# A decode kernel's output projection: from transposed 4-column matmuls to row-major accumulation with padded stationary activations

## The chip, the cores and the metric

One core of a Trainium2 chip. The metric is device microseconds of one execution. A kernel runs several times; the text gives medians, and for comparisons a ratio, explained with the result.

Abbreviations of the profile: PE is TensorE (matmuls), PEld its weight loads, DVE VectorE, ACT ScalarE, POOL GpSimd, SP the engine whose queue issues nearly all transfers. "L526" is a source line of the kernel concerned, so the same operation has another number in another kernel: the PV matmuls are L526 before and L521 after. A stretch on TensorE is called cold where its granted clock was 0.5 and warm where it was 1.0: the 512-column PV matmuls were 427 ns apart cold and 215 warm.

## The reference, cut to what matters

One decode step for 4 sequences: attention over a window of 2048 cached positions (32 query heads on 16 cached heads of 128), its output projection, and beside it an MLP with a layer norm, all added to the input.

```python
def reference(A_x, A_k_cache, A_v_cache, A_wq, A_wo, B_x, B_w1, B_w2, B_w3, B_w4):
    xn = _layernorm(A_x)
    # A: q = xn @ wq; scores over the last 2048 of 8192 positions; softmax; o = p @ v
    a = o.reshape(4, 1, 32 * 128) @ A_wo              # [4, 4096] @ [4096, 576]
    # B, for S == 1: x1 = xn (the shifted parts are all padding)
    h2 = gelu(_layernorm(xn) @ B_w3) @ B_w4           # [4, 4608] @ [4608, 576]
    return A_x + a + xn + h2
```

With one position per sequence the token shift of B moves everything out, so w1 and w2 drop out of the result. What is left is about 87 MB of K, V and weights to read for very little arithmetic.

## The kernel before

K tiles are transposed on TensorE and multiplied with q; the softmax is done once per sequence; V tiles are multiplied with the probabilities, in batches of four heads ("PV batches", 512 columns; the last two batches of the last sequence have two heads, 256 columns). In the last sequence, where there is no further K to load, the w3, wo and w4 work runs between the PV batches.

The two products that end the kernel, `@ wo` and `@ w4`, add into one PSUM tile `accT` of the *transposed* result: a 128x128 piece of the weight is stationary, and the four activation columns stream past it. For each head or w4 chunk that is five matmuls, because 576 output columns are cut into pieces of 128:

```python
def pe_wo(h0, h1):
    for h in range(h0, h1):
        PE.wait(("wo", h // HPW))
        ...
        for dc, (c0, rows) in enumerate(DCH):          # five pieces of 128 of the 576 columns
            PE.op(lambda e, ...: e.matmul(
                out=accT[:, dc * B:(dc + 1) * B], lhsT=wo_sb[:, h * D + c0:h * D + c0 + 128],
                rhs=oT_sb[:, h * B:(h + 1) * B], ...))
# at the end: copy accT to SBUF, transpose it on TensorE in fp32, add the residual (xpx20), two output DMAs
```

Transfers go through one in-order queue. K and V land in rings of slots; a V load waits until the PV batch that last used its slot is done:

```python
NKS = 8                                # K slots
NVS = 12                               # V slots; one load fills two
...
if G >= ngr:                           # ngr = NVS // 2
    DQ.wait((which + "free", G - ngr))
sp_dma(dst, src, sems[G % ngr], key=(which + "ld", G))
```

The end of the last sequence is a list of steps in program order: a PV batch, then for the batch before it the `oT` step through VectorE and its `pe_wo`, then a group of w3 matmuls; after the last PV batch the six w4 blocks.

## Time and profile before

| | before |
|---|---|
| median of the first 4 runs | 236.9 us (235.74 to 239.19) |
| median of 16 runs, those known after the prediction included | 235.8 us |
| span of the execution shown by the profile | 235.8 us (its run took 237.65) |
| TensorE busy | 189.1 us, 80% |
| VectorE, ScalarE, GpSimd busy | 37%, 27%, 2% |
| moved by DMA | 87.6 MB, mean 372 GB/s |

A span is what the profile of one execution covers; the time of that run is some 1.7 to 1.9 us longer. The lines of the profile are in the prediction.

### The profile page before, as it was taken

The numbers are of one execution on the slowest core, as the hardware profiler recorded it, in microseconds if no ns is written. First come the engines' busy times: TensorE is split into PE (matmuls) and PEld (weight loads), VectorE is DVE, ScalarE is ACT, GpSimd is POOL, SyncE is SP. The second block draws the span as 40 slices with busy tenths as digits, with TensorE's granted clock in tenths as the row PEclk, the third lists the DMA queues.
The fourth block names the chain that finished last, engine by engine and source line by source line (L and its number), as shares of the span: only waits on it lengthen the run. The fifth ranks groups of instructions, "written<-read, shape, count | busy, mean of one in ns | idle before, by whom it ended". The sixth has DMA issues, their size and how long they took to land.

```text
span 235.8 us, 6622 instructions
## 1 busy us (share of the span) xinstructions
PE 189.1 (80%) x3091; PEld 147.1 (62%) x3091; DVE 87.4 (37%) x208; ACT 63.8 (27%) x67; POOL 5.4 (2%) x9
## 2 busy tenths in 40 slices
PE   0399778779979597799999759999984595797885
PEld 0299778766857485668769447768662342536674
DVE  4435334552543425517437342536434110202110
ACT  7234253641531330415225043225221200000000
POOL 8000000000000000000000000000000000000000
PEclk9999889988999978789999985999998578757575
DMA  6999999999999999999999999999999999999960
GB/s 205 382 366 378 382 350 396 411 409 406 408 409 407 405 404 409 408 409 409 407 406 400 410 408 410 407 407 409 405 397 336 346 349 343 369 361 375 338 225 4
DMA packets 31240, 87.61 MB, mean 372 GB/s; under 512 B 1496, under 2 KB 10220, under 8 KB 31212
## 3 DMA queue, kind: packets, MB, share of 16 engines
q1 hardware_dynamic: 31196, 87.18, 98.1%
q8 instruction: 24, 0.39, 0.7%
q14 instruction: 4, 0.03, 0.0%
q10 hardware_dynamic: 16, 0.01, 0.0%
HBM read 87.17 MB, written 0.00 MB: 370 GB/s over the span
## 4 chain that ended last, share of the span: by engine, by line
PE 48%; DMA 34%; DVE 9%; SPq 4%; ACT 3%; issue 1%; ACTq 0%
DMA k_ring<-in_A_k_cache_dram 20%; PE pvb_ps L526 18%; PE ktp L455 17%; DMA v_ring<-in_A_v_cache_dram 8%; DMA wA<-in_A_wq_dram 6%; PE st_ps L496 5%; SPq L274 4%; DVE otmp L541 4%; PE st_ps L594 2%; DVE kt_sb L468 2%; PE st_ps L574 2%; PE st_ps L427 1%; DVE part_sb L683 1%; ACT L331 1%; ACT L299 1%
## 5 line engine op out<-in xcount | busy, mean ns | idle before, releaser
L455 PE MATMUL ktp<-ident_bf,k_ring 128*128 128x128 bf16 x1024 | 86.5, 235 | 6.3 <-DMA k_ring<-in_A_k_cache_dram 5.6
L473 ACT ACTIVATE kt_sb<-ktp 128x1024 bf16<-128x1024 bf16 x51 | 52.1, 1024 | 93.8 <-PE ktp L455 93.8
L526 PE MATMUL pvb_ps<-v_ring,pT_sb 128*128 128x512 bf16 (+1 forms) x272 | 69.0, 417 | 5.2 <-DMA v_ring<-in_A_v_cache_dram 5.2
L455 PEld LDWEIGHTS ktp<-ident_bf,k_ring 128*128 128x128 bf16 x1024 | 67.0, 105 | 9.6 <-DMA k_ring<-in_A_k_cache_dram 5.9
L468 DVE COPY kt_sb<-ktp 128x1024 bf16<-128x1024 bf16 x77 | 52.5, 690 | 41.2 <-PE ktp L455 41.1
L526 PEld LDWEIGHTS pvb_ps<-v_ring,pT_sb 128*128 128x128 bf16 x272 | 28.7, 110 | 37.8 <-issue 15.5
L496 PE MATMUL st_ps<-qT_sb,kt_sb 128*128 128x2 bf16 x1024 | 44.5, 165 | 2.8 <-ACT kt_sb L473 2.3
L541 DVE TENSOR_SCALAR otmp<-pvb_ps,rrs 128x128 bf16<-128x128 f32 x64 | 18.1, 344 | 77.0 <-PE pvb_ps L526 72.2
L496 PEld LDWEIGHTS st_ps<-qT_sb,kt_sb 128*128 128x128 bf16 x1024 | 40.1, 99 | 5.0 <-ACT kt_sb L473 2.7
L615 ACT ACTIVATE gT_sb<-ktp 128x36 bf16<-128x36 f32 x4 | 0.8, 201 | 32.2 <-PE ktp L610 32.2
L654 ACT ACTIVATE pT_sb<-st_ps 128x512 bf16<-128x512 f32 x4 | 2.4, 597 | 23.7 <-PE st_ps L678 23.7
L574 PE MATMUL st_ps<-oT_sb,wo_sb 128*128 128x4 bf16 x160 | 4.9, 165 | 4.2 <-DVE oT_sb L559 4.2
L574 PEld LDWEIGHTS st_ps<-oT_sb,wo_sb 128*128 128x128 bf16 x160 | 4.4, 98 | 4.6 <-DVE oT_sb L559 4.6
L352 PE MATMUL misc_ps<-ident_bf,xn_pad 128*128 128x128 bf16 x5 | 0.7, 302 | 8.2 <-DVE xn_pad L335 8.2
L686 PE MATMUL misc_ps<-ones_f,part_sb 128*128 128x1 f32 x8 | 1.9, 312 | 5.6 <-DVE part_sb L683 5.6
L554 PE MATMUL misc_ps<-imask,otmp 128*128 128x8 bf16 (+1 forms) x64 | 4.2, 168 | 2.5 <-DVE otmp L541 2.5
L610 PE MATMUL ktp<-uT_sb,wA 128*128 128x4 bf16 x180 | 5.3, 165 | 0.5 <-DMA wA<-in_B_w_dram 0.5
L610 PEld LDWEIGHTS ktp<-uT_sb,wA 128*128 128x128 bf16 x180 | 5.1, 101 | 0.8 <-issue 0.5
L686 PEld LDWEIGHTS misc_ps<-ones_f,part_sb 128*128 128x128 f32 x8 | 1.6, 250 | 6.4 <-DVE part_sb L683 6.4
L352 PEld LDWEIGHTS misc_ps<-ident_bf,xn_pad 128*128 128x128 bf16 x5 | 0.5, 129 | 8.2 <-issue 8.2
L554 PEld LDWEIGHTS misc_ps<-imask,otmp 128*128 128x128 bf16 x64 | 3.3, 100 | 3.5 <-DVE otmp L541 2.8
L683 DVE TENSOR_REDUCE part_sb<-pT_sb 128x32 f32<-128x512 bf16 x4 | 4.0, 1000 | 1.3 <-ACT pT_sb L654 1.3
(69 smaller groups left out, 54.8 us busy)
## 6 DMA issues: line engine op xcount, KB each, us to landing
k_ring<-in_A_k_cache_dram SPq DMA_DIRECT2D x32, 1024.0 KB, 15.2
v_ring<-in_A_v_cache_dram SPq DMA_DIRECT2D x32, 1024.0 KB, 17.7
wo_sb<-in_A_wo_dram SPq DMA_DIRECT2D x4, 1152.0 KB, 19.2
wA<-in_B_w_dram SPq DMA_DIRECT2D x4, 1152.0 KB, 15.4
wA<-in_A_wq_dram SPq DMA_DIRECT2D x4, 1024.0 KB, 12.0
k_ring<-in_B_w_dram SPq DMA_DIRECT2D x2, 1296.0 KB, 16.4
k_ring<-in_B_w_dram SPq DMA_DIRECT2D x1, 1440.0 KB, 18.4
kt_sb<-in_B_w_dram SPq DMA_DIRECT2D x1, 720.0 KB, 11.3
```

Source lines behind the costliest of these rows:

```text
L274: DQ.ops.append(("op", lambda e, o=out_ap, i=in_ap, s=s: e.dma_start(o, i).then_inc(s, 16), False))
L455: PE.op(lambda e, tt=tt, t=t, src=src, bank=bank: e.transpose(out=bank[:, tt * 128:(tt + 1) * 128], in_=src[:, t * 128:(t + 1) * 128], ide ...
L468: DVE.op(lambda e: e.tensor_copy(out=dst, in_=src), mark=("evac", c))
L473: ACT.op(lambda e: e.activation(out=dst, in_=src, func=ACTF.Copy), mark=("evac", c))
L496: PE.op(lambda e, t=t, src=src, hl0=hl0, b=b, stb=stb, st0=(first_of_b and tt == 0): e.matmul(out=stb[:, t * HL + hl0:t * HL + hl0 + REP], ...
L526: PE.op(lambda e, t=t, vs0=vs0, npr=npr, bank=bank: e.matmul(out=bank[:, 0:npr * 128], lhsT=pT_sb[:, t, :], rhs=v_ring[:, vs0:vs0 + npr, t ...
L541: DVE.op(lambda e, jj=jj, j=j, bank=bank: e.tensor_scalar(out=otmp[:, j, :], in0=bank[:, jj * 128:(jj + 1) * 128], scalar1=rrs32[:, 0:1], ...
L554: PE.op(lambda e, j=j, jj=jj, c0=c0, c1=c1, npr=npr: e.matmul(out=misc[:, OTF + c0:OTF + c1], lhsT=otmp[:, j, :], rhs=imask[:, j, c0:c1], ...
L574: PE.op(lambda e, h=h, dc=dc, c0=c0, st0=st0: e.matmul(out=accT[:, dc * B:(dc + 1) * B], lhsT=wo_sb[:, h * D + c0:h * D + c0 + 128], rhs=o ...
L594: PE.op(lambda e, fc=fc, dc=dc, c0=c0, last=last, st0=st0: e.matmul(out=accT[:, dc * B:(dc + 1) * B], lhsT=w4_chunk(fc, c0, 128), rhs=gT_s ...
L610: PE.op(lambda e, ff=ff, fc=fc, dc=dc, bank=bank: e.matmul(out=bank[:, ff * B:(ff + 1) * B], lhsT=wA[:, dc, fc * 128:(fc + 1) * 128], rhs= ...
L683: DVE.op(lambda e: e.tensor_reduce(out=part_sb[:, 0:HL], in_=pT_sb[:, :, 0:HL].rearrange("p t h -> p h t"), axis=AX.X, op=ALU.add), mark=( ...
```

## The change

Its intent: keep the activation stationary and let the weight stream. One head then takes two matmuls of 288 columns instead of five weight loads with 4 columns each, the result comes out in row order, and the final transpose goes. So that the stationary operand is a full 128 columns, the 4 activation columns are padded with zeros; the pads take 17 KB a partition, and the V ring pays for them.

```diff
-    NVS = 12 if NP >= 12 else NP
+    NVS = 8 if NP >= 8 else NP
...
+    DH0 = ((D + 1) // 2 + 31) // 32 * 32 if D > 512 else D
+    ACC_SPLIT = [(0, min(D, DH0))] + ([(DH0, D)] if D > DH0 else [])      # 0:288, 288:576
...
-        oT_sb = ent(nc.sbuf_tensor("oT_sb", [128, HQ * B], BF))
-        gT_sb = ent(nc.sbuf_tensor("gT_sb", [128, FC * B], BF))
+        oT_pad = ent(nc.sbuf_tensor("oT_pad", [128, HQ, 128], BF))
+        gT_pad = ent(nc.sbuf_tensor("gT_pad", [128, FC, 128], BF))
...
+        POOL.op(lambda e: e.memset(oT_pad[:, :, :], 0.0))
+        POOL.op(lambda e: e.memset(gT_pad[:, :, :], 0.0), mark="pmem")
...
-                for dc, (c0, rows) in enumerate(DCH):
-                    PE.op(... out=accT[:, dc * B:(dc + 1) * B], lhsT=wo_sb[:, h * D + c0:h * D + c0 + 128],
-                              rhs=oT_sb[:, h * B:(h + 1) * B] ...)
+                acc_mm(oT_pad[:, h, :], lambda n0, n1, h=h: wo_sb[:, h * D + n0:h * D + n1], False)
...
-            NHB = min(3, NKB)
+        NHB = NKB - 1                                     # banks for the w3 matmuls
...
-        DVE.op(... tensor_copy(out=accT_sb ...)); PE.op(... transpose ...); DVE.op(... add xpx20 ...)
+        for ai, (n0, n1) in enumerate(ACC_SPLIT):
+            DVE.op(... tensor_tensor(out=out_sb[:, n0:n1], in0=accs[ai][0:B, 0:n1 - n0], in1=xpx[:, n0:n1], op=ALU.add))
+        tiny_dma(out.rearrange("b s d -> (b s) d"), out_sb[:, :], s_out, key="out")
```

Cut: five small DMAs that brought the residual into the transposed layout, the memsets of tiles that no longer exist, and waits on the neighbouring wo or w4 block, which a 128-wide piece of the last 64 columns used to read into.

More of the change, by code (lines that the diff above doesn't have):

```diff
@@ L135, in bass_parallel_sum__sliding_block_cached__mixer_s_mlp__decode_kernel @@
     KT_ELEMS = NKT * NT * 128
-    NW4A = min(FC, (KR_ELEMS - 128) // D)
+    NW4A = min(FC, KR_ELEMS // D)
     NW4B = FC - NW4A
-    W4_SEP = not (NW4B * D + 128 <= KT_ELEMS or NW4B == 0)
+    W4_SEP = not (NW4B * D <= KT_ELEMS or NW4B == 0)
     if W4_SEP:
@@ L165, in bass_parallel_sum__sliding_block_cached__mixer_s_mlp__decode_kernel @@
     WA_COLS = max(HQ * DH, F)
+    DH0 = ((D + 1) // 2 + 31) // 32 * 32 if D > 512 else D
+    ACC_SPLIT = [(0, min(D, DH0))] + ([(DH0, D)] if D > DH0 else [])
+    assert all(n1 - n0 <= 512 for n0, n1 in ACC_SPLIT)
     def chunk_info(c):
@@ L186, in bass_parallel_sum__sliding_block_cached__mixer_s_mlp__decode_kernel @@
         wA = ent(nc.sbuf_tensor("wA", [128, NDC, WA_COLS], BF))
-        wo_sb = ent(nc.sbuf_tensor("wo_sb", [128, HQ * D + 128], BF))
+        wo_sb = ent(nc.sbuf_tensor("wo_sb", [128, HQ * D], BF))
         ident_bf = ent(nc.sbuf_tensor("ident_bf", [128, 128], BF))
         ones_bf = ent(nc.sbuf_tensor("ones_bf", [128, 128], BF))
-        ident_f = ent(nc.sbuf_tensor("ident_f", [128, 128], F32))
         identrep = ent(nc.sbuf_tensor("identrep", [128, NT * HL], BF))
@@ L195, in bass_parallel_sum__sliding_block_cached__mixer_s_mlp__decode_kernel @@
         xpx = ent(nc.sbuf_tensor("xpx", [B, D], F32))
-        xpx20 = ent(nc.sbuf_tensor("xpx20", [NR, 128], F32))
         bst1 = ent(nc.sbuf_tensor("bst1", [B, 12], F32))
@@ L216, in bass_parallel_sum__sliding_block_cached__mixer_s_mlp__decode_kernel @@
         imask = ent(nc.sbuf_tensor("imask", [128, HKV, 128], BF))
-        oT_sb = ent(nc.sbuf_tensor("oT_sb", [128, HQ * B], BF))
-        gT_sb = ent(nc.sbuf_tensor("gT_sb", [128, FC * B], BF))
-        accT_sb = ent(nc.sbuf_tensor("accT_sb", [128, 128], F32))
-        out20 = ent(nc.sbuf_tensor("out20", [NR, 128], BF))
-        w4_buf = ent(nc.sbuf_tensor("w4_buf", [128, FC * D + 128], BF)) if W4_SEP else None
+        oT_pad = ent(nc.sbuf_tensor("oT_pad", [128, HQ, 128], BF))
+        gT_pad = ent(nc.sbuf_tensor("gT_pad", [128, FC, 128], BF))
+        out_sb = ent(nc.sbuf_tensor("out_sb", [B, D], BF))
+        w4_buf = ent(nc.sbuf_tensor("w4_buf", [128, FC * D], BF)) if W4_SEP else None
         ktp = [ent(nc.psum_tensor("ktp%d" % i, [128, 1024], BF)) for i in range(NKB)]
@@ L230, in bass_parallel_sum__sliding_block_cached__mixer_s_mlp__decode_kernel @@
         ktp_f = [t[:, :].bitcast(F32) for t in ktp]
-        accT = st[B % 2]
-        outT = ktp_f[NKB - 1]
+        accs = [st[B % 2][:, :], ktp_f[NKB - 1]]
+        NHB = NKB - 1
+        assert NHB >= 1 and len(ACC_SPLIT) <= len(accs)
         assert NDC * 128 <= 1024
@@ L251, in bass_parallel_sum__sliding_block_cached__mixer_s_mlp__decode_kernel @@
         s_pe, s_dve, s_act, s_pool = sem("c_pe"), sem("c_dve"), sem("c_act"), sem("c_pool")
-        s_x, s_out, s_xpx = sem("d_x"), sem("d_out"), sem("d_xpx")
+        s_x, s_out = sem("d_x"), sem("d_out")
         s_wq = [sem("d_wq%d" % i) for i in range(NQB)]
@@ L291, in bass_parallel_sum__sliding_block_cached__mixer_s_mlp__decode_kernel @@
         DVE.op(lambda e: e.memset(rrs32[:, :], 0.0))
-        DVE.op(lambda e: e.memset(negm_bc[:, :], 0.0))
-        DVE.op(lambda e: e.memset(accT_sb[:, :], 0.0))
-        DVE.op(lambda e: e.memset(xpx20[:, :], 0.0))
-        if W4_SEP:
-            DVE.op(lambda e: e.memset(w4_buf[:, FC * D:FC * D + 128], 0.0))
-        DVE.selfsync(lambda e: e.memset(wo_sb[:, HQ * D:HQ * D + 128], 0.0), "dmem")
+        DVE.selfsync(lambda e: e.memset(negm_bc[:, :], 0.0), "dmem")
         if REM > 0:
@@ L309, in bass_parallel_sum__sliding_block_cached__mixer_s_mlp__decode_kernel @@
             mark="identrep")
-        POOL.op(lambda e: e.affine_select(
-            out=ident_f[:, :], in_=ones_bf[:, :], pattern=[[1, 128]],
-            compare_op=ALU.is_equal, fill=0.0, base=0, channel_multiplier=-1), mark="identf")
         POOL.wait("identbf")
@@ L558, in pe_oTacc, with acc_mm @@
             DVE.wait(("oTacc", n))
+            DVE.wait("pmem")
             DVE.op(lambda e, b=b, c0=c0, c1=c1: e.tensor_copy(
-                out=oT_sb[:, :].rearrange("p (h b) -> p h b", b=B)[:, c0:c1, b], in_=misc[:, OTF + c0:OTF + c1]),
-                mark=("oTb", n))
-        acc_started = [False]
+                out=oT_pad[:, c0:c1, b], in_=misc[:, OTF + c0:OTF + c1]), mark=("oTb", n))
+        acc_started = [False] * len(ACC_SPLIT)
+        def acc_mm(lhsT, rhs_fn, last):
+            for ai, (n0, n1) in enumerate(ACC_SPLIT):
+                st0 = not acc_started[ai]
+                acc_started[ai] = True
+                fin = last and ai == len(ACC_SPLIT) - 1
+                PE.op(lambda e, ai=ai, n0=n0, n1=n1, st0=st0, fin=fin: e.matmul(
+                    out=accs[ai][:, 0:n1 - n0], lhsT=lhsT, rhs=rhs_fn(n0, n1), start=st0, stop=fin,
+                    skip_group_check=True), mark=("acc" if fin else None))
         def pe_wo(h0, h1):
-            PE.wait("dmem")
+            PE.wait("pmem")
             for h in range(h0, h1):
                 PE.wait(("wo", h // HPW))
-                if REM > 0 and h + 1 < HQ:
-                    PE.wait(("wo", (h + 1) // HPW))
-                for dc, (c0, rows) in enumerate(DCH):
-                    st0 = not acc_started[0]
-                    acc_started[0] = True
-                    PE.op(lambda e, h=h, dc=dc, c0=c0, st0=st0: e.matmul(
-                        out=accT[:, dc * B:(dc + 1) * B], lhsT=wo_sb[:, h * D + c0:h * D + c0 + 128],
-                        rhs=oT_sb[:, h * B:(h + 1) * B], start=st0, stop=False, skip_group_check=True))
-        blk_of_fc = {}
-        for i_, (region_, f0_, n_) in enumerate(w4_blocks):
-            for fc_ in range(f0_, f0_ + n_):
-                blk_of_fc[fc_] = i_
+                acc_mm(oT_pad[:, h, :], lambda n0, n1, h=h: wo_sb[:, h * D + n0:h * D + n1], False)
         def pe_w4mm(i, last_block):
@@ L585, in pe_w4mm @@
             PE.wait(("w4", i))
+            PE.wait("pmem")
             for fc in range(f0, f0 + n):
                 PE.wait(("gelu", fc // FPB))
-                if REM > 0 and fc + 1 < FC and w4_blocks[blk_of_fc[fc + 1]][0] == region:
-                    PE.wait(("w4", blk_of_fc[fc + 1]))
-                for dc, (c0, rows) in enumerate(DCH):
-                    last = (last_block and fc == f0 + n - 1 and dc == NDC - 1)
-                    st0 = not acc_started[0]
-                    acc_started[0] = True
-                    PE.op(lambda e, fc=fc, dc=dc, c0=c0, last=last, st0=st0: e.matmul(
-                        out=accT[:, dc * B:(dc + 1) * B], lhsT=w4_chunk(fc, c0, 128),
-                        rhs=gT_sb[:, fc * B:(fc + 1) * B], start=st0, stop=last, skip_group_check=True),
-                        mark=("acc" if last else None))
+                acc_mm(gT_pad[:, fc, :], lambda n0, n1, fc=fc: w4_chunk(fc, n0, n1 - n0),
+                       last_block and fc == f0 + n - 1)
         def pe_h2T(j):
@@ L614, in pe_h2T @@
             ACT.wait(("h2T", j))
-            ACT.op(lambda e, j=j, bank=bank: e.activation(out=gT_sb[:, j * FPB * B:(j + 1) * FPB * B],
-                                                          in_=bank[:, 0:FPB * B], func=ACTF.Gelu_apprx_tanh),
-                   mark=("gelu", j))
+            ACT.wait("pmem")
+            ACT.op(lambda e, j=j, bank=bank: e.activation(
+                out=gT_pad[:, j * FPB:(j + 1) * FPB, 0:B], in_=bank[:, 0:FPB * B].rearrange("p (f b) -> p f b", b=B),
+                func=ACTF.Gelu_apprx_tanh), mark=("gelu", j))
         q_done = set()
@@ L661, in bass_parallel_sum__sliding_block_cached__mixer_s_mlp__decode_kernel @@
                     dma_wo(j)
-            if b == 0:
-                SP.wait("xpx")
-                SP.wait("dmem")
-                for dc, (c0, rows) in enumerate(DCH):
-                    tiny_dma(xpx20[dc * B:(dc + 1) * B, 0:rows], xpx[:, c0:c0 + rows], s_xpx)
-                EV["xpx20"] = (s_xpx, 16 * dma_counts[s_xpx.num])
             g0_chunks = list(range(c1_lo, c1_lo + CPG)) if nxt else []
@@ L761, in bass_parallel_sum__sliding_block_cached__mixer_s_mlp__decode_kernel @@
         DVE.wait("acc")
-        DVE.op(lambda e: e.tensor_copy(out=accT_sb[:, 0:NR], in_=accT[:, 0:NR]), mark="accTsb")
-        PE.wait("accTsb")
-        PE.wait("identf")
-        PE.op(lambda e: e.transpose(out=outT[:, 0:128], in_=accT_sb[:, :], identity=ident_f[:, :]), mark="outT")
-        DVE.wait("outT")
-        DVE.wait("xpx20")
-        DVE.op(lambda e: e.tensor_tensor(out=out20[:, :], in0=outT[0:NR, 0:128], in1=xpx20[:, :], op=ALU.add),
-               mark="fin")
-        SP.wait("fin")
-        out2 = out.rearrange("b s d -> (b s) d")
-        if NFULL > 0:
-            tiny_dma(out2[:, 0:NFULL * 128].rearrange("b (c p) -> c b p", p=128), out20[0:NFULL * B, :], s_out)
-        if REM > 0:
-            ACT.wait("fin")
-            act_dma(out2[:, NFULL * 128:D], out20[NFULL * B:NR, 0:REM], s_out)
-        EV["out"] = (s_out, 16 * dma_counts[s_out.num])
+        for ai, (n0, n1) in enumerate(ACC_SPLIT):
+            DVE.op(lambda e, ai=ai, n0=n0, n1=n1: e.tensor_tensor(
+                out=out_sb[:, n0:n1], in0=accs[ai][0:B, 0:n1 - n0], in1=xpx[:, n0:n1], op=ALU.add),
+                mark=("fin" if ai == len(ACC_SPLIT) - 1 else None))
+        SP.wait("fin")
+        tiny_dma(out.rearrange("b s d -> (b s) d"), out_sb[:, :], s_out, key="out")
         SP.wait("out")
```

## The prediction

> **What bounds the kernel now.** I read the page's slices first, then the chain of waits for the last 48 us, then a table of stretches cut at the PV batches, then the issue queue's order of time.
>
> ```profile
> PEclk9999889988999978789999985999998578757575
> DMA  6999999999999999999999999999999999999960
> GB/s 205 382 366 378 382 350 396 411 409 406 408 409 407 405 404 409 408 409 409 407 406 400 410 408 410 407 407 409 405 397 336 346 349 343 369 361 375 338 225 4
> ```
>
> Transfers are saturated in every slice from 6 us to about 224 us: some 408 GB/s while K and V stream, 336 to 375 in the last batch, where w3, wo and w4 share the queue. Until there the loads set the pace. Only the last slices are different, and there the clock reads 5 to 8.
>
> ```profile
> 188.11 18.50 DMA v_ring<-in_A_v_cache_dram
> 206.60 0.14 issue
> 206.74 6.10 PE pvb_ps L526 x16
> 212.84 0.02 issue
> 212.86 1.13 DVE otmp L541 x4
> 213.99 0.09 DVE oT_sb L559
> ...
> 226.15 0.66 PE st_ps L574 x20
> 226.80 1.25 PE st_ps L594 x50
> ...
> 228.37 0.66 PE st_ps L574 x20
> 229.03 3.48 PE st_ps L594 x130
> 232.51 0.02 issue
> 232.53 0.19 DVE accT_sb L762
> 232.72 0.04 issue
> 232.76 0.49 PE ktp L765
> 233.25 0.02 issue
> 233.28 0.28 DVE out L768
> ```
>
> The last wait on a load ends at 206.60. From there to 232.51 the chain is TensorE with short VectorE hand-overs, never a load: the last three w4 blocks land at about 228.3, 229.0 and 229.5 (issue plus time to landing), ahead of their use at 231.3. So the tail is TensorE's, 25.9 us, plus 3.3 us of epilogue. Whatever the change adds to TensorE here is paid in full; before 206 there is slack.
>
> ```profile
> 197.07:202.40 5.33, 5.33 (x20) 2.15 (x20) 0.00 (x0) 0.00 (x0) 0.00 (x0) 0.68 1.04 355
> 202.40:206.70 4.30, 2.40 (x88) 2.26 (x85) 1.21 (x5) 0.20 (x1) 0.00 (x0) 0.80 1.04 368
> 206.74:212.80 6.06, 6.06 (x20) 2.31 (x20) 0.00 (x0) 0.00 (x0) 0.00 (x0) 0.58 1.03 362
> 216.30:219.90 3.60, 3.60 (x27) 2.60 (x24) 0.00 (x0) 0.20 (x1) 0.00 (x0) 0.50 1.08 350
> 221.80:225.40 3.60, 3.60 (x23) 2.52 (x20) 0.00 (x0) 0.00 (x0) 0.00 (x0) 0.50 1.07 380
> 228.30:232.50 4.20, 4.13 (x150) 4.04 (x150) 0.01 (x1) 0.00 (x0) 0.00 (x0) 0.56 0.06 18
> ```
>
> The third number from the right is the granted clock. All three PV batches of the chain run mostly at half clock (512 columns every 427 ns, 256 columns every 213 ns), though TensorE reads busy. In the last row it reads 98% busy with 4-column matmuls, yet sits at 0.56.
>
> [...] the weight loads of the PV batches change from 0.43 us apart to dense at about 191.2, 201.5 and 211.8, 10.3 us apart[...]. The clock stayed full after the window 191.2 to 194.6 with 1.5 us of PV in it (44%), fell after 201.5 to 204.9 and 211.8 to 215.2 with 0.9 to 1.0 us (about 28%), and did not rise after 215.2 to 218.6 with 2.3 us (67%). [...]
>
> [...] full-clock PV batches elsewhere take 3.61 us for 16, the last of them 0.38, so 3.23/15 = 215 ns each[...].
>
> **The change, part by part.**
>
> (a) Output projection and w4. Now each of 32 heads and 36 w4 chunks takes five weight-swapping matmuls of 4 columns: 1.15 us for 40 is 28.8 ns each, 0.144 us a head; 3.48 for 130 is 26.8 ns each, 0.134 us a chunk. Afterwards each takes two of 288 columns: 0.245 us warm, 0.48 cold. After 206.6 lie 24 heads and 36 chunks: now 1.15+1.23+0.66+1.25+0.66+3.48 = 8.4 us; afterwards 14.7 warm (+6.3) or 28.8 cold (+20.4). It is fewer instructions (136 for 340) but far more columns.
>
> (b) What gives some of it back[...]. Walking the tail forward with (a)[...]: the first 8 heads start at 203.7, still warm, end 205.6; w3 matmuls (1.25) to 206.9; window 201.5 to 204.9 then holds 0.9 PV + 1.2 heads = 62%, and 204.9 to 208.35 holds 0.7 + 1.45 = 64%: the clock stays up. The PV batch takes 3.45 instead of 6.1, to 210.4; VectorE hand-over 1.3; 8 heads 1.96 to 213.7; w3 1.25 to 214.9; PV of 256 columns 1.75 instead of 3.45 to 216.7; hand-over 0.75; 8 heads to 219.4; PV 1.75 to 221.1; 0.75; 4 heads 0.98 to 222.9; w4 ten chunks 2.45 to 225.3; 0.3; 4 heads to 226.6; 26 chunks 6.37 to 233.0, plus some 0.25 for the last to drain: 233.2 against 232.5. The three PV batches repay 2.65+1.7+1.7 = 6.05 of 6.3; the first heads push the start by 0.3. So +0.7 if the clock holds throughout.
>
> (c) Epilogue. The copy, the fp32 transpose and the add go: 232.51 to 233.56 is 1.05 us. In their place two adds of 4x288. The present 20x128 add takes 0.279 and an early 4x576 add 0.693, about 1.0 ns a column plus 0.1 to 0.15: some 0.4 each, about 0.8 together. -0.25 us. One output transfer replaces two side by side: nothing.
>
> (d) V ring 12 to 8 slots. V group G then waits for the PV batch holding group G-4, not G-6. Comparing each V issue with the PV ends, the worst delays are at batch starts: 96.72 becomes 105.8 (+9.1) and 139.19 becomes 149.6 (+10.4); in the last batch 187.11 becomes 192.9 and 196.79 becomes 202.4. But the K transfer issued just before lands at 96.31+14.6 = 110.9 and 138.78+16.1 = 154.9, so 5 us of backlog remains at both. Transfers that were queued anyway start no later. Expected cost 0, on thin margins.
>
> (e) Removed: the five small xpx copies (7.93 us of the issue queue at 29.6, when the DMA engines are full: 0); four short VectorE memsets (0.11 to 0.17 us each, during startup: 0). Added: two GpSimd memsets, 4096 and 4608 elements; by its 2.0 us for 2048 elements, some 8.5 us after its present 6.5, ready near 15 us, first used near 60: 0. Two h2T banks instead of three: the wait is on a gelu one whole PV batch old: 0.
>
> Sum, clock held: +0.7 - 0.25, near +0.5 us.
>
> **Rivals.** First, the clock does not hold. For: it is half in four of the rows above[...]. If the 206.7 batch alone runs cold, +2.6; if everything does, nothing is repaid and the tail grows by the full 20.4. Against: the walk shows 60 to 64% in each window, well above the 44% that held. Since the walk has no margin elsewhere, I allow an average of 1 us for cold spells. Second, the ring starves the DMA engines at a batch start: 5 us of backlog has to cover the start-up of the new transfers, which no row isolates; I take each failure at 1 to 3 us, a fraction of that backlog, and the two last-batch delays could move the 206.6 landing. For it: K transfers queue in order behind the delayed V. Against: the backlog just counted; about one in five. Third, fewer, wider instructions simply being faster: the tail falls onto the DMA end, near 229.5 plus epilogue, -2 us or so. Against: 14.7 us of columns can't beat 8.4 even at full clock; only more PV savings than (b) counts could, and (b) takes all of them.
>
> **Range and chances.** From 236.9: +0.5 for the held clock, +0.8 for cold spells on average, +0.3 for the ring: 238.5. Low end 235.8: the held case with a little luck and run-to-run spread. High end 242.5: two cold batches and one starved transition. The 2% limits are 232.2 and 241.6; the lower needs more than the tail has to give: 0.03. The upper needs over 4.7 us, a largely cold tail or ring trouble: 0.17. Within: 0.80.
>
> **What would show it.** Granted clock near 1.0 from about 208 us to the end and the last three PV batches at 3.5, 1.75 and 1.75 us confirm (b); 288-column matmuls 122 ns apart confirm (a). DMA slices all 9 and PV's wait for V still ending near 206.6 confirm (d); a 7 or 8 in the slices near 105 or 150 us, or a V issue waiting on L526 followed by TensorE waiting on a load, refutes it. The prediction fails slow if the final 26 chunks take 12 us (cold), and fails fast if the accumulation ends before 231.

## The result, and the profile after

| | before | after |
|---|---|---|
| median, fast and slow runs | 235.79 us (16 runs) | 239.03 us (11 runs) |
| ratio of fast runs | 1 | 1.0143, 95% interval 1.0107 to 1.0179 |

A ratio here is the mean time of one kernel's fast runs over the mean of the other's fast runs of the same rounds, so it is not quite the ratio of the medians. The change made the kernel 1.4% slower, 3.4 us. That is within the 2% which the prediction called "same", and 239.0 is within its range. But the prediction's own step was +1.6 us (238.5 from 236.9), half of what was measured, so its terms have to be gone through.

The slices of the kernel after (40 equal parts of the span; clock in tenths of full speed, DMA share in tenths, rate):

```profile
PEclk9999999775899999799999997999979575899999
DMA  6999999999899999999999999999999999999920
GB/s 205 381 353 370 375 340 392 408 410 408 334 391 373 382 406 408 411 406 408 410 405 396 413 408 410 407 407 413 400 399 333 340 363 347 364 360 385 381 95 1
```

Two things differ from before. The clock is full in the last five slices, where before it read 5 or 7. And there is an 8 in the DMA row, in the eleventh slice (60 to 66 us), with 334 GB/s where its neighbours have 408 and 391.

The chain of waits of the kernel after (start, length, what), from the last wait on a load:

```profile
182.31 17.33 DMA v_ring<-in_A_v_cache_dram
199.63 0.14 issue
199.77 6.31 PE pvb_ps L521 x16
...
210.63 3.49 PE pvb_ps L521 x16
...
218.68 1.78 PE pvb_ps L521 x16
...
223.38 1.75 PE pvb_ps L521 x16
...
237.22 0.14 PE ktp L565
237.36 0.02 issue
237.38 0.45 DVE out_sb L742
237.83 0.36 DVEq L183
```

The last wait for V is one PV batch earlier in the program than before. From 199.63 on TensorE is the bound without a break. The three last PV batches take 3.49, 1.78 and 1.75 us, where the chain before had 6.10, 3.45 and 3.44. What is left out are the 288-column matmuls, each 0.12 us long in the chain.

The order of time of the first microseconds holds a surprise (start, length, engine, line, operation, tile, shape):

```profile
6.09 3.51 POOL L314 MEMSET oT_pad<- 128x4096 bf16 x1
...
7.61 6.02 DVE L330 TENSOR_SCALAR xn_pad<-x_sb,mv,rstd 4x576 bf16<-4x576 bf16 x1
9.53 3.94 POOL L315 MEMSET gT_pad<- 128x4608 bf16 x1
```

Before, the same VectorE instruction took 0.42 us:

```profile
7.63 0.42 DVE L335 TENSOR_SCALAR xn_pad<-x_sb,mv,rstd 4x576 bf16<-4x576 bf16 x1
```

Now it starts while GpSimd writes zeros and ends just after GpSimd is done; it waits out both memsets, though the second begins 1.9 us after it. TensorE waits for it: its second group of input transposes started at 10.3 us before and 15.9 after.

Both profiles are of executions listed as slow, so I compare them with each other and don't put their difference down to the change: 235.8 against 239.9 us of span is 4.1 us, more than the 3.4 of the ratio. Cut at two points, the start of the last-but-one 512-column PV batch (197.07 and 199.77) and the end of the accumulation (232.53 and 237.38), it is +2.7 us in front, 37.6 against 35.5 = +2.1 between, and 2.5 against 3.3 = -0.8 for the epilogue.

### The profile page after: what moved, and what is told of

Its sections match the earlier page's. It is cut to its first block, busy times and chain, and to the rows that moved or that the text cites. A ratio compares the mean times of both kernels' runs of the same rounds, so it can differ in the third digit from the quotient of the medians.

```text
span 239.9 us, 6207 instructions
## 1 busy us (share of the span) xinstructions
PE 190.0 (79%) x2886; PEld 147.7 (62%) x2886; DVE 93.1 (39%) x205; ACT 63.7 (27%) x67; POOL 12.5 (5%) x10
## 4 chain that ended last, share of the span: by engine, by line
PE 62%; DMA 19%; DVE 12%; ACT 3%; issue 3%; SPq 0%; ACTq 0%; DVEq 0%
PE ktp L450 22%; PE pvb_ps L521 21%; DMA k_ring<-in_A_k_cache_dram 11%; DMA v_ring<-in_A_v_cache_dram 7%; PE st_ps L491 7%; PE st_ps L565 4%; DVE otmp L536 4%; PE ktp L565 3%; DVE xn_pad L330 3%; DVE kt_sb L463 2%; DVE part_sb L662 1%; PE st_ps L422 1%; PE ktp L594 1%; ACT kt_sb L468 1%; DVE pm_sb L630 1%
## 5 line engine op out<-in xcount | busy, mean ns | idle before, releaser
L450 PE MATMUL ktp<-ident_bf,k_ring 128*128 128x128 bf16 x1024 | 85.6, 233 | 6.7 <-DMA k_ring<-in_A_k_cache_dram 4.8
L521 PE MATMUL pvb_ps<-v_ring,pT_sb 128*128 128x512 bf16 (+1 forms) x272 | 64.3, 393 | 3.5 <-DMA v_ring<-in_A_v_cache_dram 3.5
L521 PEld LDWEIGHTS pvb_ps<-v_ring,pT_sb 128*128 128x128 bf16 x272 | 26.8, 103 | 33.6 <-issue 12.3
L565 PE MATMUL st_ps<-wo_sb,oT_pad 128*128 128x288 bf16 x32 | 8.1, 288 | 4.2 <-DVE oT_pad L555 4.2
L600 ACT ACTIVATE gT_pad<-ktp 128x36 bf16<-128x36 f32 x4 | 0.8, 201 | 30.5 <-PE ktp L594 30.5
L565 PE MATMUL ktp<-wo_sb,oT_pad 128*128 128x288 bf16 x32 | 8.0, 286 | 0.0
L565 PE MATMUL st_ps<-k_ring,gT_pad 128*128 128x288 bf16 x28 | 6.9, 286 | 0.0
L565 PE MATMUL ktp<-k_ring,gT_pad 128*128 128x288 bf16 x28 | 6.9, 286 | 0.0
L565 PEld LDWEIGHTS st_ps<-wo_sb,oT_pad 128*128 128x128 bf16 x32 | 3.1, 97 | 5.4 <-DVE oT_pad L555 4.7
L330 DVE TENSOR_SCALAR xn_pad<-x_sb,mv,rstd 4x576 bf16<-4x576 bf16 x1 | 6.0, 6019 | 0.0
## 6 DMA issues: line engine op xcount, KB each, us to landing
kt_sb<-in_B_w_dram SPq DMA_DIRECT2D x1, 720.0 KB, 11.1
```

The costliest lines, as they stand in the source:

```text
L330: DVE.selfsync(lambda e: e.tensor_scalar(out=xn_bf, in0=x_sb[:, :], scalar1=mv1[:, 0:1], scalar2=rstd1[:, 0:1], op0=ALU.subtract, op1=ALU. ...
L450: PE.op(lambda e, tt=tt, t=t, src=src, bank=bank: e.transpose(out=bank[:, tt * 128:(tt + 1) * 128], in_=src[:, t * 128:(t + 1) * 128], ide ...
L521: PE.op(lambda e, t=t, vs0=vs0, npr=npr, bank=bank: e.matmul(out=bank[:, 0:npr * 128], lhsT=pT_sb[:, t, :], rhs=v_ring[:, vs0:vs0 + npr, t ...
L565: PE.op(lambda e, ai=ai, n0=n0, n1=n1, st0=st0, fin=fin: e.matmul(out=accs[ai][:, 0:n1 - n0], lhsT=lhsT, rhs=rhs_fn(n0, n1), start=st0, st ...
```

## The experiments

The theory after the traces, called "stall times ring" below: the memsets block VectorE, TensorE starts some 5 us late, and a V ring of 8 can't absorb that, so that the DMA engines run dry near 65 us; the tail itself costs little. The rivals: the ring alone does it; or the new tail itself costs the 3 us. Twelve runs were made in all, two of them second traces of the unedited kernels (single runs). Where the 2 us windows are named, they are a table of the DMA share in each window from 6 to 224 us.

### a_defer: the memsets after the layer norms

```diff
+        POOL.wait("xT")
         POOL.op(lambda e: e.memset(oT_pad[:, :, :], 0.0))
```

> The changed kernel with one edit: GpSimd's two zeroing memsets wait until VectorE has finished both layer norms. Theory (stall times ring): in the changed kernel VectorE's scale to xn_pad took 6.02 us instead of 0.43 while the memsets ran, TensorE began its work 5.6 us later, and with a V ring of 8 that lateness emptied the DMA engines near 65 us; without it the 64 to 66 us hole goes, the landing that TensorE waits for in the last batch moves back from 199.8 to about 197, and the time falls by 2 to 3 us, to a ratio of 1.000 to 1.006. Rival (the ring of 8 alone starves the DMA engines, and the late start was absorbed): xn_pad is back at 0.4 us but the hole stays, ratio 1.012 to 1.016 as for the changed kernel.

Measured: ratio 1.0095 (1.0041 to 1.0148). xn_pad took 0.42 us again, and the hole was gone: one window at 0.93 (106 us), all others at 0.97 or above, 77.7 MB moved by 200 us against 76.7 in the profile of the kernel after. But only about a third of the loss went with it. The intervals overlap, so that third is not settled by this run alone.

### c_ring12_defer: also the V ring of 12

```diff
-    NVS = 8 if NP >= 8 else NP
+    NVS = 12 if NP >= 12 else NP
-        gT_pad = ent(nc.sbuf_tensor("gT_pad", [128, FC, 128], BF))
+        gT_pad = ent(nc.sbuf_tensor("gT_pad", [128, FC, 64], BF))
```

> As a_defer, and the V ring is 12 slots again, made to fit by padding the gelu output to 64 columns instead of 128. It isolates the new projection, its clock and the epilogue. Theory (stall times ring): same as a_defer within 0.4%, ratio 0.998 to 1.006, because a ring of 8 without a late start costs nothing. Rival (ring alone): 2 us or more below a_defer. A third reading, that the new tail itself costs the 3 us: ratio 1.01 or more here.

Measured: ratio 1.0113 (1.0058 to 1.0167), no window below 0.97. With neither a stall nor a small ring the kernel is still 1.1% slower than before. The third reading is the one that fits: most of the loss is in the new tail. The theory that the tail costs little fell here.

### d_before_ring8 and e_before_ring8_stall: ring and stall in the kernel before

The ring alone, then with GpSimd memsets on V slots that are not loaded yet, at the place where the change has its memsets:

```diff
-    NVS = 12 if NP >= 12 else NP
+    NVS = 8 if NP >= 8 else NP
...                                                     # e_before_ring8_stall only:
+        POOL.op(lambda e: e.memset(v_ring[:, NVS - 4:NVS - 2, :], 0.0))
+        POOL.op(lambda e: e.memset(v_ring[:, NVS - 2:NVS, :], 0.0))
+        POOL.op(lambda e: e.memset(junk[:, :], 0.0), mark="jmem")       # 512 elements
```

The V loads wait for these memsets (that line is cut); the issue queue's list of waits shows none on GpSimd.

> The kernel before with a V ring of 8 slots and nothing else. Theory (stall times ring): V issues come later by up to 10 us but the DMA engines stay full, ratio 0.997 to 1.004. Rival (ring alone): a hole in the DMA share in the first batch, ratio 1.008 to 1.015.

Measured: ratio 1.0041 (0.9983 to 1.0098); apart from the start (0.95 at 6 us) no window below 0.97. The ring alone makes no hole.

> The kernel before with a V ring of 8 slots and, at the place of the new memsets, three GpSimd memsets of 8704 elements in all (on V slots not yet loaded). Theory (stall times ring): xn_pad takes 5 to 6 us, the hole near 65 us appears, ratio 1.008 to 1.014. Rival (ring alone): like d_before_ring8. If the late start has no part in it either, ratio near 1.00.

Measured: ratio 1.0098 (1.0044 to 1.0152), xn_pad 6.29 us. The stall is reproduced in the old kernel. But the hole near 65 us was not: instead there are dips at 24, 26, 32 and 36 us (0.94, 0.88, 0.95, 0.93), besides 0.96 at 6 and 0.94 at 210 us. K loads went out late there: the pair that was issued at 16.20 us in the first trace of before and at 15.77 in d_before_ring8 was issued at 21.74 here.

### s_before_stall: the stall with the ring of 12

The same memsets in the kernel before, ring unchanged.

> The kernel before with its V ring of 12 and the same three GpSimd memsets as e_before_ring8_stall. Theory (it takes both the stall and the small ring to starve the DMA engines): xn_pad takes 5 to 6 us, but the DMA share stays at 0.97 or above in all 2 us windows from 8 to 224 us, ratio 0.997 to 1.004. Rival (the stall alone): ratio 1.005 to 1.012, with windows below 0.97.

Measured: ratio 1.0062 (1.0006 to 1.0117), xn_pad 6.29 us, windows at 26 and 32 us with a DMA share of 0.81 and 0.92 (besides 0.95 at 6 and 0.94 at 218 us). The rival was right: the stall needs no small ring to leave the DMA engines short of work for a moment. What comes late is the refill of the K ring, 8 slots in every kernel here: the pair of K loads named above went out at 21.96 us.

### b_ring12_stall: the fourth corner in the changed kernel

```diff
-    NVS = 8 if NP >= 8 else NP
+    NVS = 12 if NP >= 12 else NP
-        gT_pad = ent(nc.sbuf_tensor("gT_pad", [128, FC, 128], BF))
+        gT_pad = ent(nc.sbuf_tensor("gT_pad", [128, FC, 64], BF))
+        POOL.op(lambda e: e.memset(v_ring[:, NVS - 1, :], 0.0))
         POOL.op(lambda e: e.memset(oT_pad[:, :, :], 0.0))
```

Here too the V loads wait for the memsets (cut).

> The changed kernel with the V ring back at 12 (gelu output padded to 64 columns, as in c_ring12_defer) and the memsets where the change put them, one more of 2048 elements on an unloaded V slot making up for the smaller one. It is the fourth corner of ring and stall. Theory (stall times ring): the 64 us hole is gone; what stays of the stall are short dips between 24 and 36 us as in s_before_stall; ratio 1.009 to 1.014, that is within 0.3% of c_ring12_defer's 1.0113 and below the changed kernel's 1.0143. Rival (the stall alone makes the loss): as the changed kernel, 1.013 to 1.018.

Measured: ratio 1.0113 (1.006 to 1.0166), xn_pad 5.83 us, dips of 0.85 at 26 and 0.88 at 32 us (besides 0.94 at 6), no hole near 64. As the theory had it within its range; but the kernel without the stall, c_ring12_defer, has the same ratio, so this pair shows no cost of the stall.

### after_again: a second trace of the changed kernel

No edit.

> The changed kernel, unedited, for a second trace. Theory (the hole belongs to the kernel, not to one execution): xn_pad takes about 6 us again, and in the first batch some 2 us window between 55 and 80 us shows a DMA share below 0.9 while a V issue waits for the first PV batch; megabytes moved by 200 us are 0.6 to 1.2 below those of a_defer (77.7). Rival (the hole was chance): every window from 8 to 224 us is at 0.97 or above.

Measured: 238.48 us, span 236.7. xn_pad took 6.01 us again, but the window at 64 us was full:

```profile
26.00:28.00 2.00, 2.00 (x52) 2.00 (x51) 1.34 (x2) 1.08 (x2) 0.00 (x0) 1.00 0.91 301
...
64.00:66.00 2.00, 2.00 (x52) 2.00 (x51) 1.15 (x3) 1.02 (x1) 0.00 (x0) 1.00 1.02 403
```

The last three numbers of a row are clock, DMA share and GB/s. In the first trace the row of 64 to 66 us had 0.47 and 186. The rival was right on the hole: it is not there in every execution. (Its "every window at 0.97 or above" did not hold: 0.91 at 26, 0.92 at 32 and 0.96 at 152 us.) It is a near miss that one execution made: the K load before the waiting V load went out at 54.29 us there and the V load at 64.89, 10.6 us later; here it was 52.32 and 61.85, 9.5 us, and the transfers in flight lasted. The 77.5 MB moved by 200 us lie just short of a_defer's 77.7.

### before_again: a second trace of the kernel before

No edit.

> The kernel before, unedited, for a second trace. The prediction read how much the clock could repay from one execution whose span, 235.8 us, was some 2 us above the median span of the later executions of before (233.9). Theory: the execution read was one in which all three last PV batches ran mostly cold, and another execution shows at least one of them at full clock and a tail shorter by 1.7 to 3 us from the last V wait to the end. Rival: the tail is the same in every execution and the difference lies in the transfers, that is in when the last V group lands.

Measured: 236.51 us, span 234.7. The end of its chain of waits:

```profile
221.93 8.56 DMA kt_sb<-in_B_w_dram
230.50 0.05 issue
230.54 0.81 PE st_ps L594 x20
...
231.38 0.19 DVE accT_sb L762
```

In this execution the tail of before ends on a load, the last w4 block, at 230.50. The PV batch at 207.42 still took 5.25 us, but the next two took 1.91 each at full clock:

```profile
216.13 1.91 PE L526 MATMUL pvb_ps<-v_ring,pT_sb 128*128 128x256 bf16 x16
...
219.84 1.91 PE L526 MATMUL pvb_ps<-v_ring,pT_sb 128*128 128x256 bf16 x16
```

TensorE came to the w4 blocks early enough to wait for them. From the start of the batch at 207.42 to the end of the span it took 27.2 us, against 29.1 from 206.74 in the first trace. So the theory held for this execution: the one that the prediction read was one in which the last two batches ran cold (3.58 each), and there TensorE was the bound of the tail and the loads had slack. Here the loads are the bound, and TensorE waits for w4 for 0.32, 1.01 and 0.32 us.

Of the five traces with the old tail and no added matmuls, this one alone has both 256-column batches warm; d_before_ring8 has one, the other three none (2.49 to 3.58 us), and none of the others ends on a load. In d_before_ring8, e_before_ring8_stall and s_before_stall TensorE stands for 1.42, 0.20 and 1.30 us between w4 matmuls too, but the profile calls that "issue", so it shows nothing that was waited for, and it comes after the 67th of the last 130 of these matmuls in all three (here d_before_ring8):

```profile
227.69 1.79 PE st_ps L594 x67
229.47 1.42 issue
230.89 1.83 PE st_ps L594 x63
```

A pause at a fixed place in the instruction stream is not a wait for a load of weights. The packed traces point to what it is. They keep the times of the packets of 16384 B that bring instructions (`q8 instruction: 24` in the profile page's list of DMA queues). In these three traces and in g_before_fill below, such a packet ends 1.44, 1.38, 1.37 and 1.30 us before the first matmul after the pause. In the two traces of before that matmul starts 1.84 and 1.60 us after the packet, and there is no pause. So TensorE probably waits for its next instructions; that is read from times alone, and no run tests it. The six traces with row-major accumulation, which has fewer instructions, have 22 such packets, none in the last 11 us before the accumulation ends, and no such pause.

### f_unpadded: no padding at all

```diff
-        oT_pad = ent(nc.sbuf_tensor("oT_pad", [128, HQ, 128], BF))
-        gT_pad = ent(nc.sbuf_tensor("gT_pad", [128, FC, 128], BF))
+        oT_pad = ent(nc.sbuf_tensor("oT_pad", [128, HQ, B], BF))
+        gT_pad = ent(nc.sbuf_tensor("gT_pad", [128, FC, B], BF))
-                    out=accs[ai][:, 0:n1 - n0], ...
+                    out=accs[ai][0:B, 0:n1 - n0], ...
```

and no memsets, no waits on them, ring of 12.

> The changed kernel with no padding: 4 stationary columns instead of 128, no memsets, V ring of 12. It asks whether the padding has a part in the speed or in the clock. Theory (the clock counts streaming, not occupied columns): matmuls of 288 columns 122 ns apart, clock full from about 208 us on, ratio as for c_ring12_defer, 1.006 to 1.014. Rival (a nearly empty array counts as idle): the clock falls as with the 4-column matmuls of before, 240 ns apart, tail longer by 8 us or more, ratio above 1.03.

Measured: ratio 1.0084 (1.0037 to 1.0131), correct. Its clock by slices, and one of its last two PV batches in the order of time:

```profile
PEclk9999797989999959889999955999998587999999
```

```profile
214.35 1.91 PE L519 MATMUL pvb_ps<-v_ring,pT_sb 128*128 128x256 bf16 x16
```

Clock 9 to the end and 1.91 us for the batch with 4 stationary columns, matmuls 0.12 us apart. The padding was needed for neither speed nor clock. Everything that it cost (17 KB, the ring, the memsets) bought nothing. It is also a second estimate of what the new tail costs by itself: 0.8%, beside the 1.1% of c_ring12_defer.

### g_before_fill: wide matmuls for the clock alone

If wide matmuls hold the clock, the kernel before can have that without the new layout: 512-column matmuls into a PSUM bank that is free by then, where TensorE waits for VectorE anyway.

```diff
+        def pe_fill(k):
+            for _ in range(k):
+                PE.op(lambda e: e.matmul(out=st[(B - 1) % 2][:, 0:512], lhsT=ident_bf[:, :],
+                                         rhs=pT_sb[:, 0:4, :], start=True, stop=True))
...
                         pe_oTacc(m)
+                        pe_fill(fill)             # 6 after a 512-column batch, 3 after a 256-column one, 1 last
                         PE.wait(("oTb", m))
...
+                    if g >= 3 and per_g.get(g, []):
+                        pe_fill(2)                # ahead of two groups of w3 matmuls
```

> The kernel before, with 21 matmuls of 512 columns whose result nobody reads put in the last batch where TensorE waits for VectorE (and two before each of two groups of w3 matmuls). It tests whether wide matmuls alone hold the clock in the tail of before. Theory: the PV batches of the tail take 3.5, 1.75 and 1.75 us in every trace, TensorE reaches the w4 blocks about 5 us earlier and waits there for their landing near 229 us; the end moves to the DMA floor, ratio 0.988 to 0.998. Rival (the clock in the tail is set by something other than matmul activity): the batches stay cold and the fill costs time, ratio 1.005 or more.

Measured: ratio 0.9957 (0.9905 to 1.0009). There were 23 such matmuls, not the 21 of the text. The two 256-column batches took 1.91 us; the 512-column batch at 206.67 was cold in this trace, 6.34 us, after a wait for V, so "in every trace" was wrong. The wait for w4 that I expected is not shown: TensorE stood 1.96 us at 227.35, but as "issue", after the 44th of the last 130 w4 matmuls. That is 23 earlier than the pause described under before_again, by as many as the added matmuls are, so it is the same place in the instruction stream. The accumulation ended at 231.76, close to the 231.38 of before_again: the cold batch and the pause took what the two warm batches gave. The interval includes 1.

### h_fill_wide: longer packets for w3 and w4

On top of g_before_fill, w3 in two loads with 4608-byte rows, and w4 with consecutive rows in one partition:

```diff
-            sp_dma(dst.rearrange("p (c n) -> p c n", n=D),
-                   B_w4[f0 * 128:(f0 + n) * 128, :].rearrange("(c p) n -> p c n", p=128), ...)
+            sp_dma(dst, B_w4[f0 * 128:(f0 + n) * 128, :].rearrange("(p c) n -> p (c n)", p=128), ...)
...
-                        lhsT=wA[:, dc, fc * 128:(fc + 1) * 128],
+                        lhsT=wA[:, dc, c:c + 127 * n + 1:n],       # c = f0 * 128 + fc - f0
```

Cut from this edit: three of the four w3 groups also move one V group later, and the largest w4 block goes from first to third place (the latter in j_fill_w4 too). So it is not packet length alone.

> g_before_fill with longer packets: w3 in two loads of 4608 byte rows instead of four of 2304, and w4 with each partition taking consecutive rows (5 to 11 KB a packet instead of 1152 B), the w3 columns read with a step to match. It tests the reading that the tail of before ends on the last w4 landing, so that neither faster nor slower TensorE work is worth more than its 1 to 2 us of slack there. Theory: the GB/s of the slices from 176 us on rise from 336 to 375 to near 400, the last w4 block lands 3 to 4 us earlier, ratio 0.978 to 0.990. Rival (these loads are slow for another reason than packet length): rates unchanged, ratio 0.993 to 1.000.

Measured: ratio 1.0105 (1.0056 to 1.0153), worse. The window table (engine busy times, then clock, DMA share, GB/s) tells the two loads apart:

```profile
200.00:206.00 6.00, 5.92 (x63) 2.79 (x60) 1.21 (x5) 0.00 (x0) 0.00 (x0) 0.87 1.02 305
212.00:218.00 6.00, 6.00 (x25) 2.26 (x23) 1.21 (x5) 0.00 (x0) 0.00 (x0) 0.73 1.03 430
```

The w4 blocks, in packets of 10 and 11 KB, moved in a stretch of 430 GB/s; the stretch at 200 us, in which the second w3 load was in flight (issued at 182.32), had 305 with the DMA engines just as busy. In the trace of before, as busy, K and V packets of 4096 B moved at some 408 GB/s, and the last batch, with packets of 1152 and 2304 B among them, at 336 to 375. These stretches differ in more than packet size. That the w3 rows are the cause is inferred from the overlap, and no run here settles why they would be. The second w3 load also landed only at 208.4 us, with everything on TensorE queued behind its matmuls. And the w3 weights that are read with a step cost more: 45 weight-load-and-matmul pairs took about 2.8 us instead of 1.28.

### j_fill_w4: long packets for half of w4

Only the first two w4 blocks get the long packets; their stepped w3 matmuls fall where TensorE waits for V.

```diff
+            if i < 2:
+                sp_dma(dst, B_w4[f0 * 128:(f0 + n) * 128, :].rearrange("(p c) n -> p (c n)", p=128), ...)
+                return
```

> g_before_fill with only the first two w4 blocks (9 chunks each) loaded in long packets, whose stepped w3 columns are used while TensorE waits for V anyway; w3 is loaded as before. In h_fill_wide the w4 slices rose to 405 and 429 GB/s, but the longer w3 loads moved only 293 and 300 and held up the w3 matmuls, so the first part is kept and the second dropped. Theory (the tail of before ends on the last w4 landing): half of w4 at some 410 GB/s instead of 360 saves about 0.9 us there, ratio 0.988 to 0.996. Rival: TensorE is late for another reason and the ratio stays that of g_before_fill, 0.9957, or above.

Measured: ratio 0.9945 (0.9914 to 0.9977), median 234.87 us in 9 runs. Its chain of waits ends like that of before_again, 1.3 us earlier:

```profile
220.28 8.94 DMA kt_sb<-in_B_w_dram
229.22 0.05 issue
229.26 0.81 PE st_ps L598 x20
```

The four PV batches took 5.30, 3.61, 1.91 and 1.91 us here. The two groups of 45 pairs of weight load and 4-column matmul that read w3 with a step of 9 took 2.83 and 2.81 us, the two with a step of 1 took 1.28 and 1.27. This version beats both kernels: the one before by 0.55%, with an interval clear of 1, and the changed one by about 2% (0.9945 / 1.0143 = 0.980, from two ratios). It is the kernel before with its transposed accumulation; the row-major layout is not in it. Beside g_before_fill's 0.9957 (0.9905 to 1.0009) the difference is inside the intervals, so it is not shown that the long packets add anything to the wide matmuls.

## Why the prediction was right or wrong

**The bound ("from there to 232.51 the chain is TensorE, never a load").** True of the execution that was read, but not of every one: before_again ends on the last w4 load, with two of the three last batches warm. So one trace of the old tail was not the right thing to subtract from.

**(a) More columns.** Right to the digit. In every trace with this layout the last 288-column matmuls are 122 to 123 ns apart at the median. The 0.245 us for two was the estimate; 288/512 of the 215 ns measured for 512 columns gives 121 ns for one.

**(b) The clock repays 6.05 us of 6.3.** Direction right, size wrong. That the clock would stay up with wide matmuls in 62 and 64% of a stretch was the estimate. It rests on four stretches of one trace: the clock was 1.00 after the one with 44% (194.6 to 198.0 us), 0.51 and 0.50 after the two with about 28% (204.9 to 208.35 and 215.2 to 218.6), and 0.50 after the one with 67% (218.6 to 222.0). The stretches are as long as the steps of the clock in that trace: the packed trace has it at 1.0 or 0.5, for 3.41 us or a multiple of that each time but the last. What the clock follows is not shown: 4-column matmuls, 98% busy, ran at 0.56 there (228.3 to 232.5 us), but in h_fill_wide, 100% busy, at 1.00 (230 to 232 us).

The clock held in all six traces with row-major accumulation (two of the kernel after, a_defer, b_ring12_stall, c_ring12_defer, f_unpadded): the last three PV batches took 3.61, 1.91 and 1.91 us in the order of time, every time to 0.01. But from the start of the 512-column PV batch near 197 us to the end of the accumulation the prediction's walk takes 36.1 us (197.07 to 233.2), and these six traces take 37.6, 37.7, 37.9, 38.1, 37.0 and 36.9 us, mean 37.5; five with the old tail and no fill take 35.5, 33.6, 35.2, 35.2 and 35.0, mean 34.9, their pauses on TensorE included (37.5 and 34.7 without the two slow executions). That is +2.6 us where the sum had +0.7.

Of the difference, 0.6 us is on the old side: the credit was counted against an execution with every late batch mostly cold, and two traces of five have one or two warm. The larger part, 1.4 us, is on the new side, and 0.8 of it comes before the stretch for which (b) expected the clock to hold. The last two 512-column batches, before and after:

```profile
197.07 5.30 PE L526 MATMUL pvb_ps<-v_ring,pT_sb 128*128 128x512 bf16 x16 [3.05 <-DMA v_ring<-in_A_v_cache_dram]
206.74 6.09 PE L526 MATMUL pvb_ps<-v_ring,pT_sb 128*128 128x512 bf16 x16 [0.72 <-DMA v_ring<-in_A_v_cache_dram]
```

```profile
199.77 6.30 PE L521 MATMUL pvb_ps<-v_ring,pT_sb 128*128 128x512 bf16 x16 [2.50 <-DMA v_ring<-in_A_v_cache_dram]
210.49 3.61 PE L521 MATMUL pvb_ps<-v_ring,pT_sb 128*128 128x512 bf16 x16
```

In four of the six traces the first of these two ran cold for longer, 6.30 to 6.53 us, and the second began 10.9 to 11.1 us after it where the walk has 9.8. In the trace that was read, TensorE stood 0.72 us waiting for V in front of the second; that was all the slack in front of it, and row-major accumulation used it up: only c_ring12_defer still waits there, 0.31 us. The other 0.6 us is spread over the steps behind. So the tail's sum is the mis-sized term: the time of the steps in front of the warm stretch, the slack that was to hide them, and the execution that the credit was read from. Why that first batch stays cold longer in four traces no run here settles.

**(c) Epilogue -0.25.** It was -0.8: the two adds took 0.81 us as estimated, but the single output transfer was also quicker, 1.7 us from the issue at 238.22 to the end of the span against 2.2 for the two of before. With it the tail is +2.6 - 0.8 = +1.8 us, 0.8%; the ratios of c_ring12_defer and f_unpadded say 1.1 and 0.8%.

**(d) The ring, "expected cost 0, on thin margins".** About right. The V loads waited for PV batches as foreseen (51.4 us of the queue's time in the kernel after, none before), and the loads in flight covered it in all traces but one. That one hole came in the first batch, not at the two later batch starts that the prediction named; near those, a_defer has a window at 0.93 (106 us) and after_again one at 0.96 (152 us), no more. Four pairs give the ring alone: 1.0041 against 1, 1.0098 against 1.0062, 1.0143 against 1.0113, and 1.0095 against 1.0113, mean +0.2%. None is clear of the noise, so the runs show no cost of the ring, nor exclude 0.5%.

**(e) The memsets, "ready near 15 us, first used near 60: 0".** Wrong in kind. Only the reader of the memsets' result was looked at, not what VectorE does while GpSimd writes. The `tensor_scalar` that starts during the memsets took 6.02 us instead of 0.42 in the kernel after, and 5.83 to 6.29 in all five traces with memsets there; where they wait it took 0.42. A `reciprocal` of 4x1 that started at 7.42 us, during the first memset, took 0.15 us, as in the trace of before. No run here settles why the one is held and the other is not. The delay puts TensorE's start 5.6 us back, and in four of the five traces that have it the DMA share dips near 26 and 32 us. In time, four pairs give 1.0143 against 1.0095, 1.0113 against 1.0113, 1.0062 against 1 and 1.0098 against 1.0041, mean +0.4%, or 1 us; only s_before_stall is clear of 1 by itself, and just so.

Put together, +1.0% for the tail (the mean of 1.13 and 0.84), +0.4 for the stall and +0.2 for the ring make 1.6%, beside 1.43 measured. The time of 238.5 came out close to 239.0 partly because two errors met: the base of 236.9 was 1.1 us above the later median, and the step was about half of the true one. (The step also took the average of 1 us for cold spells as 0.8.)

**The rivals.** "The clock does not hold" did not happen once. "The ring starves the DMA engines" happened in one trace of two. "Fewer, wider instructions simply being faster" did not. The rival that was missing: that in another execution the old tail holds the clock by itself, and ends on the w4 loads.

## What to carry to other kernels

Look at more than one execution before counting a saving against it: here the last two PV batches took 3.58 us each in one trace of the kernel before and 1.91 in the next, and with them the bound of the tail changed. A transfer with little slack behind the bound on the page is the next bound, so a credit on the engine in front of it is worth no more than that slack. Work "off the critical path" on GpSimd should be checked against the VectorE instructions that run beside it: here a `tensor_scalar` on the path took 6.02 us instead of 0.42 during two memsets. And padding a stationary operand with zeros should be tried without the padding first.
